# Turning f, q and k in separate parts, and one partial sum read by ScalarE: a change to a gated linear attention with an MLP on one core

## The chip, the cores and the metric

The kernel runs as one program on one core of a Trainium2 chip. The metric is the device time of one execution in microseconds; shorter is better. The core has five engines that run beside each other and wait for each other by semaphores: TensorE (PE in the profile, with PEld for its weight loads), VectorE (DVE), ScalarE (ACT), GpSimd (POOL) and SyncE (SP), which issues the transfers. Each engine works through its own list of instructions in order.

## The reference

```python
# q, k, v, f_logit: 4 batches x 8 heads x 768 tokens x 48
f = 1.0 / (1.0 + np.exp(-f_logit))
for t in range(S):
    state = f[:, :, t, :, None] * state + np.einsum('bhd,bhe->bhde', k[:, :, t], v[:, :, t])
    y[:, :, t] = np.einsum('bhd,bhde->bhe', q[:, :, t], state)
x = y.transpose(0, 2, 1, 3).reshape(B * S, H * D)     # 3072 tokens x 384
h = x @ w_in                                          # 384 x 2048
g = h * (1.0 / (1.0 + np.exp(-1.702 * h)))
out = g @ w_out                                       # 2048 x 384
```

Everything is float32.

## The kernel before

**Units.** The 3072 tokens are cut into 12 units of 256 tokens, three to a batch; the state is carried along within a batch. The attention of unit n+1 is computed while the MLP of earlier units runs. The MLP work lies in a list, `fill`, and `merge(n, fill, ...)` emits the parts of unit n's attention one after the other and, behind each part, as much of `fill` as the part's `share` says. A part kind with a share of 3 out of 19 is followed by 3/19 of that merge's MLP columns. In the merges 2 and 3 the same is done with the rest of the weights, which arrive as raw bits and are rebuilt by VectorE and ScalarE (`convert`, lines 208 to 228); there `converting` says how many of these instructions follow a part.

**A unit's attention.** For unit n >= 3 the inputs f, q and k of a unit come into the tile `raw` as they lie in memory. VectorE turns each of them (`turn`, line 327): f into `F`, on which ScalarE then computes the sigmoid (line 332), q into one of two places in `X`, k into the third place of `X`. `begin_f`, `begin` and `begin_k` do this; each then lets SyncE fetch the next unit's input (line 258). `begin` also has two small GpSimd copies (lines 357 and 358). `begin_k` has four instructions more: ScalarE copies half of k and half of q aside (`set_aside`, line 423, tiles `Kc` and `Qc`), VectorE multiplies the other halves in place by the gates (`promote`, line 439), and ScalarE copies the next `Kc`. `begin_gates` multiplies gates into `tot` on GpSimd (line 376); it has to wait for the previous unit's states, because `tot` is one buffer.

The parts of a unit in their order are: three parts "V" (scores of two levels each on TensorE, line 384; `promote`, masks on VectorE, line 410; the sums over v into the tile `y`, line 448), two parts "T" (k is turned back on TensorE, line 505, and copied to `kn` by ScalarE, line 506), one part "S" (the last sums into `y`, the products for the states, line 523, and the states `st` on VectorE, lines 538 to 543). The product of q with the states, line 563, is emitted at the head of the next unit's first part; its result is copied (`yT`, line 571) and sent into the MLP's input `xT`. Units 0 to 2 have six single levels "W" instead of the three "V". `parts_of(n)` places the turnings of unit n+1 among the parts of unit n.

**Who orders.** TensorE's order is that of the emission throughout. Up to the end of merge 3 the other engines' order is that of the emission too, but for instructions of later units that the scheduler puts in among the last of them. From merge 4 on a scheduler orders VectorE, ScalarE, GpSimd and SyncE.

**The MLP.** From unit 3 on, `mlp_unit` computes `h` (line 727, 16 tiles of 128 columns), the sigmoid (line 732) and the product `g` (line 733), then `mlp_o7` computes the output from seven products of quarters instead of eight. The seven products use four sums in PSUM, X, W, Y and Z, 128 x 192 each. X, Y and Z go on after they have been read once: the order is X, W, X, Y, Z, Y, Z, and p1, p4, p2, p6, p5, p7, p3 are what is done when each product is complete:

```python
def p6():
    nc.vector.tensor_tensor(row("u2"), t["p1"], t["Y"], ALU.add)
def p3():
    nc.vector.tensor_tensor(out_(0)[:, HC:], t["u2"], t["Z"], ALU.add)
    store(n, 0, out_(0))
```

The products h, o, the tkn of the parts "T" and the four sums share four PSUM buffers of the tag "mm". In the units 0 to 2 the MLP runs in blocks of four tiles: `mlp_block`, with o in line 755, its first sum copied by ScalarE (line 791) and the others added by VectorE (line 793).

Of the kernel before, what the change touches and what calls it, by code (L numbers as in the profile page):

```python
# [13 lines left out]
ALU = mybir.AluOpType  # L14
# [9 lines left out]
def kernel(  # L24
# [33 lines left out]
    nc = tc.nc  # L58
    B, H, S, D = q.shape
# [17 lines left out]
    N_FILL = 3  # L77
# [153 lines left out]
    def convert():  # L231

        if state["begin"] < len(pairs) and len(todo) <= NOP:
            begin_pair(state["begin"])
            state["begin"] += 1
        if todo and todo[0]:
            todo.pop(0)()
        if todo and todo[0] is None:
            todo.pop(0)
            state["done"] += 2  # L240
            fetch_weights()
# [34 lines left out]
    def load_vl(n, l):  # L276

        if n >= NALL:
            return
        t = vls[n, l] = ld.tile([P, DM], F32, tag=f"vl{l}", name=f"vl_{n}_{l}")  # L280
        if n < N_TURN:
            pt = ps.tile([P, DM], F32, tag="mm", name=f"tv_{n}_{l}", bufs=4)
            for g in range(NG):
                nc.tensor.matmul(
                    pt[g * 64:(g + 1) * 64], lhsT=perm[:, l - 1, :] if l else ident[:, ::2], rhs=vns[n][:, g, :],
                    start=True, stop=True,
                )
            nc.scalar.copy(t, pt)
            return
        nc.sync.dma_start(out=t, in_=v_toks[n % 2].rearrange("(n two m) e -> two n m e", two=2, m=LEV[l])[0])  # L290
# [315 lines left out]
    HF, HC = NFF // 2, DM // 2  # L606
    T = {}

    def quarter(w, i, j, ffs=slice(0, HF)):
        return w[:, i * HF + ffs.start:i * HF + ffs.stop, j * HC:(j + 1) * HC]  # L610
# [35 lines left out]
    def last_sum(n, g):  # L646

        for j in range(2):
            by = slice(0, G)
            nc.vector.tensor_tensor(g[j + 2][:, :, by], g[j + 2][:, :, by], g["S", j][:, :, by], ALU.subtract)  # L650

    def mlp_o7(n, g):
        a = lambda i, j: lambda f: g[j * 2 + f // FG][:, f % FG, i * G:(i + 1) * G]
        s = lambda i: lambda f: g["S", f // FG][:, f % FG, i * G:(i + 1) * G]
        b = lambda i, j: lambda f: quarter(w_out, i, j)[:, f]
        T_ = lambda i: lambda f: T[i][:, f] if i < 4 else T[4](f)
        t = {}

        def out_(tt):
            if "o" not in g:  # L660
                g["o"] = mlp.tile([P, U // P, DM], F32, tag="osb", name=f"osb_{n}", bufs=1)
            return g["o"][:, tt]

        def row(name):
            t[name] = mlp.tile([P, HC], F32, tag=name, name=f"{name}_{n}", bufs=1)
            return t[name]

        def p1():
            nc.scalar.copy(row("p1"), t["X"])

        def p4():
            nc.scalar.copy(row("p4"), t["W"])

        def p2():
            nc.scalar.copy(out_(0)[:, :HC], t["X"])
            last_sum(n, g)

        def p6():
            nc.vector.tensor_tensor(row("u2"), t["p1"], t["Y"], ALU.add)  # L679

        def p5():
            nc.scalar.copy(row("p5"), t["Z"])

        def p7():
            nc.vector.tensor_tensor(row("u3"), t["p1"], t["Y"], ALU.add)
            nc.vector.tensor_tensor(out_(1)[:, :HC], t["u3"], t["p4"], ALU.subtract)
            nc.vector.tensor_tensor(out_(1)[:, HC:], t["u3"], t["p5"], ALU.add)
            store(n, 1, out_(1))

        def p3():  # L690
            nc.vector.tensor_tensor(out_(0)[:, HC:], t["u2"], t["Z"], ALU.add)
            store(n, 0, out_(0))


        products = (
            ("X", a(0, 0), b(0, 0), p1, True), ("W", a(1, 1), T_(4), p4, True), ("X", a(0, 1), b(1, 0), p2, False),
            ("Y", s(0), T_(2), p6, True), ("Z", a(1, 0), T_(1), p5, True), ("Y", s(1), T_(3), p7, False),
            ("Z", a(0, 1), b(1, 1), p3, False),
        )

        def one(bank, lhs, rhs, done, new, f):
            if new and f == 0:
                t[bank] = ps.tile([P, HC], F32, tag="mm", name=f"o_{n}_{bank}", bufs=4)
            nc.tensor.matmul(  # L704
                t[bank], lhsT=lhs(f), rhs=rhs(f), start=(new and f == 0), stop=(f == HF - 1), skip_group_check=True,
            )
            if f == HF - 1:
                done()
        return [(HC, lambda p=p, f=f: one(*p, f), 0) for p in products for f in range(HF)]
# [53 lines left out]
    def store(n, tt, o):  # L763
        r0 = n * U + tt * P - 1
        nc.sync.dma_start(out=out[max(r0, 0):r0 + P, :], in_=o[1:] if r0 < 0 else o)
# [38 lines left out]
    def keep_up(times):  # L804

        if times:
            pt = ps.tile([P, NL * 64], F32, tag="mm", name=f"idle_{next(serial)}", bufs=4)
        for _ in range(times):
            nc.tensor.matmul(pt, lhsT=ident, rhs=masks.rearrange("p l t -> p (l t)"), start=True, stop=True)
# [4 lines left out]
    def parts_of(n):  # L814

        parts = list(units[n][1])
        _, inter = parts.pop()
        if n:
            kind, scores = parts[0]
            _, ahead = units[n - 1][1][-1]  # L820
            parts[0] = kind, lambda: (ahead(), scores())
        if n < N_TURN:

            def with_v(l):
                kind, fn = parts[l]
                return kind, lambda: (fn(), load_vl(n, l) if n == 0 or l else None, keep_up(2 * (n == 0 and l < 3)))
            parts[:NL] = [with_v(l) for l in range(NL)]
        if n + 1 < NALL:
            begin_f, begin, begin_k, begin_gates = units[n + 1][0]
            i = len(parts)  # L830
            if n + 1 < N_FILL:

                parts.append(("K", lambda: (begin_k(), begin_gates(), load_vl(n + 1, 0) if n + 1 < N_TURN else None)))
                parts.insert(i - 4, ("B", begin if n == 0 else lambda: None))
                parts.insert(i - 5, ("B", begin_f))
                if n:

                    kind, head = parts[0]
                    parts[0] = kind, lambda: (head(), begin())
            else:  # L840
                kind, states = parts.pop()
                parts += [("B", begin_k), (kind, lambda: (states(), begin_gates()))]
                parts.insert(i - 3, ("B", lambda: (begin_f(), begin())))
        else:
            parts.append(("W", inter))
        return parts

    def merge(n, fill, columns, share, pieces=0, hold=0, by=1.0, chores=()):

        parts = parts_of(n)
        total = sum(share(kind) for kind, _ in parts)
        converting = {"W": 3, "T": 3, "B": 1} if n < N_FILL - 1 else {"W": 3, "V": 4, "S": 3, "T": 1, "B": 1}
        total_ops = sum(converting.get(kind, 0) for kind, _ in parts)
        held = sum(share(kind) for kind, _ in parts[:hold])
        at = at_ops = done = ops = 0
        for kind, fn in parts:
            ready = state["done"]
            fn()  # L860
            for chore in chores[:2]:
                chore()
            chores = chores[2:]
            at += share(kind)
            at_ops += converting.get(kind, 0)
            n_ops = min(int(pieces * NOP * at_ops / (by * total_ops)), pieces * NOP) - ops
            ops += n_ops
            first, n_columns = done, max(0, columns * (at - held) / (total - held) - done)

            def some(end):  # L870
                nonlocal done
                while fill and done < end and fill[0][2] <= ready:
                    w, emit, _ = fill.pop(0)
                    emit()
                    done += w
            for i in range(n_ops):
                some(first + n_columns * i / n_ops)
                convert()
            some(first + n_columns)

    def steady(kind):
        return {"W": 3, "V": 4, "S": 3, "T": 1, "B": 1, "K": 1}.get(kind, 0)

    UNIT = NFF * NK * U + U // P * NFF * DM

# [12 lines left out]
    load_vn(1)  # L898
    fill = []
    merge(0, fill, 0, steady, 8)  # L900
    fill += mlp_blocks((0, 0)) + mlp_blocks((0, 1))
    merge(1, fill, UNIT // 2 - LAG // 2, steady, 10, hold=1)
# [40 lines left out]
```

## Time and profile before

| What | Value |
|---|---|
| Median of 4 runs (lowest to highest) | 658.35 us (656.14 to 659.15) |
| The profiled execution's time; its span | 658.86 us; 657.0 us |
| TensorE busy (PE) | 634.2 us, 97% of the span |
| TensorE weight loads (PEld) | 543.4 us, 83% |
| VectorE busy | 444.9 us, 68% |
| ScalarE busy | 229.9 us, 35% |
| GpSimd busy | 54.5 us, 8% |
| Mean granted TensorE clock | 0.997 |
| DMA | 67.67 MB, mean 103 GB/s |

Times in the text are microseconds from the start of the span unless they are durations. In the timeline a row has its start, the time from its first to its last instruction, the engine, the line, the operation, output and inputs, and how many instructions were merged into it; in square brackets stand the idle time of the engine before it and what ended that. Where two instructions of one engine follow each other, the second can start a little before the first one's recorded end, so the distance of two starts can be shorter than the duration. A float32 product shows as two MATMUL records.

### The profile page before, as it was taken

How to read it: one execution, taken by the hardware profiler on the slowest of the kernel's cores; microseconds unless marked ns; L12 is line 12 of the kernel's file. 1: busy time of each engine (PE TensorE's matmuls, PEld its weight loads, DVE VectorE, ACT ScalarE, POOL GpSimd, SP SyncE). 2: the span in 40 equal slices, each digit the busy share in tenths (PEclk: the TensorE clock that was granted, in tenths of full speed). 3: DMA queues.
4: the chain of work that ended last, by engine and by line, in shares of the span. 5: the costliest groups of instructions: out<-in, count | busy, mean ns of one | idle time of the engine just before them, and what ended most of it. 6: DMA issues, size and time to landing. Idle time of an engine off the chain costs nothing.

```text
span 657.0 us, 20397 instructions
## 1 busy us (share of the span) xinstructions
PE 634.2 (97%) x8958; PEld 543.4 (83%) x8958; DVE 444.9 (68%) x802; ACT 229.9 (35%) x477; POOL 54.5 (8%) x116
## 2 busy tenths in 40 slices
PE   6978989989999999999999999999999999999997
PEld 5656757766678689989989989989989989989997
DVE  2998967788887757657657658558558557553571
ACT  3465433243223423423324324324324324222120
POOL 3020020020001002002002002002002002000000
PEclk9999989999999999999999999999999999999999
DMA  8888865294125444524524524615614202101000
GB/s 185 209 220 215 208 144 130 77 222 81 44 58 153 133 107 109 149 54 118 146 46 121 143 49 120 160 31 119 166 27 103 67 25 62 40 2 26 25 1 24
DMA packets 67554, 67.67 MB, mean 103 GB/s; under 512 B 30410, under 2 KB 61290, under 8 KB 67466
## 3 DMA queue, kind: packets, MB, share of 16 engines
q1 hardware_dynamic: 67466, 66.38, 40.5%
q8 instruction: 70, 1.15, 0.8%
q14 instruction: 18, 0.15, 0.1%
HBM read 56.92 MB, written 8.65 MB: 100 GB/s over the span
## 4 chain that ended last, share of the span: by engine, by line
PE 84%; DVE 7%; DMA 5%; ACT 1%; issue 1%; SPq 1%; DVEq 0%; ACTq 0%
PE h L727 36%; PE o_Y L704 8%; PE o_X L704 7%; PE o L755 7%; PE o_Z L704 7%; PE sc L384 5%; PE y L448 4%; PE o_W L704 4%; DMA vn<-v_tok 2%; PE t L339 2%; PE y L563 2%; PE sc L523 1%; DMA bits<-in_moe_w_in_dram 1%; PE tkn L505 1%; DMA xT<-yT 1%; DVE s L219 1%
## 5 line engine op out<-in xcount | busy, mean ns | idle before, releaser
L727 PE MATMUL h<-xT,w_in 128*128 128x256 f32 (+1 forms) x1152 | 261.5, 383 | 6.8 <-DMA xT<-yT 4.2
L727 PEld LDWEIGHTS h<-xT,w_in 128*128 128x128 f32 x1152 | 216.5, 191 | 40.8 <-issue 3.9
L733 DVE TENSOR_TENSOR g<-h,sg 128x256 f32<-128x256 f32 (+1 forms) x192 | 80.9, 423 | 101.0 <-ACT sg L732 98.6
L732 ACT ACTIVATE sg<-h 128x256 f32<-128x256 f32 (+1 forms) x192 | 73.4, 384 | 195.9 <-PE h L727 190.9
L423 ACT COPY Kc<-X 128x512 f32<-128x512 f32 x69 | 46.2, 669 | 119.7 <-DVE X L439 84.8
L755 PE MATMUL o<-w_out,g 128*128 128x384 f32 x192 | 66.1, 493 | 0.0
L439 DVE TENSOR_TENSOR X<-X,tot 128x1024 f32<-128x1024 f32 x45 | 55.2, 1226 | 15.3 <-PE sc L384 10.2
L755 PEld LDWEIGHTS o<-w_out,g 128*128 128x128 f32 x192 | 35.3, 190 | 22.9 <-issue 1.4
L704 PE MATMUL o_X<-w_out,g 128*128 128x192 f32 x288 | 51.9, 329 | 0.0
L704 PE MATMUL o_Y<-T,S 128*128 128x192 f32 x288 | 51.1, 331 | 0.1
L704 PEld LDWEIGHTS o_Y<-T,S 128*128 128x128 f32 x288 | 46.5, 190 | 2.5 <-DVE u L679 1.2
L704 PEld LDWEIGHTS o_X<-w_out,g 128*128 128x128 f32 x288 | 47.3, 190 | 0.9
L410 DVE TENSOR_TENSOR A<-sc,masks 128x512 f32<-128x512 f32 x72 | 46.9, 682 | 0.0
L448 PE MATMUL y<-A,vl 64*48 64x64 f32 x2304 | 41.2, 217 | 0.5 <-issue 0.4
L376 POOL TENSOR_TENSOR tot<-F 128x512 f32<-128x512 f32 x12 | 12.5, 1040 | 348.0 <-DVE st L540 348.0
L448 PEld LDWEIGHTS y<-A,vl 64*48 64x48 f32 x2304 | 36.2, 120 | 4.0 <-issue 4.0
L327 DVE STREAM_TRANSPOSE X<-raw 128x1024 f32<-128x1024 f32 x18 | 36.7, 2039 | 2.4 <-PE y L563 2.4
L571 ACT COPY yT<-y 48x512 f32<-48x512 f32 x48 | 27.9, 580 | 12.7 <-PE y L563 12.2
L384 PEld LDWEIGHTS sc<-X,Kc 48*64 48x64 f32 x1344 | 24.1, 134 | 8.2 <-issue 3.2
L384 PE MATMUL sc<-X,Kc 48*64 48x64 f32 x1344 | 28.3, 220 | 1.8 <-DVE A L410 1.7
L376 POOL TENSOR_TENSOR tot<-tot 128x256 f32<-128x256 f32 (+4 forms) x60 | 27.1, 452 | 4.7
L704 PE MATMUL o_Z<-w_out,g 128*128 128x192 f32 x144 | 26.6, 331 | 0.0
(93 smaller groups left out, 658.4 us busy)
## 6 DMA issues: line engine op xcount, KB each, us to landing
vl<-v_tok SPq DMA_DIRECT2D x60, 192.0 KB, 3.0
bits<-in_moe_w_out_dram SPq DMA_DIRECT2D x8, 768.0 KB, 9.4
bits<-in_moe_w_in_dram SPq DMA_DIRECT2D x8, 576.0 KB, 7.8
v_tok<-in_v_dram SPq DMA_DIRECT2D x10, 384.0 KB, 4.3
vn<-v_tok SPq DMA_DIRECT2D x10, 384.0 KB, 7.1
xT<-yT SPq DMA_DIRECT2D x24, 144.0 KB, 2.8
raw<-in_q_dram SPq DMA_DIRECT2D x18, 192.0 KB, 4.2
raw<-in_f_logit_dram SPq DMA_DIRECT2D x18, 192.0 KB, 4.3
```

Source lines behind the costliest of these rows:

```text
L327: nc.vector.transpose(out.rearrange("p (a i j) -> p a j i", a=NP, j=R), raw[:, j].rearrange("p a (j d) -> p (a j) d", j=R)[:, :, :32],)
L376: nc.gpsimd.tensor_tensor(tn, t2[:, :, 0], t2[:, :, 1], ALU.mult)
L384: nc.tensor.matmul(out[g * HS:(g + 1) * HS, h, a, :], lhsT=lhs(h, a * U + g * G), rhs=rhs(h, a * U + g * G), start=True, stop=True,)
L410: nc.vector.tensor_tensor(A[:, :, c:c + w].rearrange("p h (x t) -> p h x t", t=64), t["sc"][:, :, c:c + w].rearrange("p h (x t) -> p h x t ...
L423: nc.scalar.copy(c.rearrange("p (n m) -> p n m", m=m), X[:, j, :NA].rearrange("p (n two m) -> p n two m", two=2, m=m)[:, :, hf, :],)
L439: nc.vector.tensor_tensor(qk, qk, by, ALU.mult)
L448: nc.tensor.matmul(dst(h, g, a), lhsT=vls[n, u][g * 64:(g + 1) * 64, (2 * a + h) * D:(2 * a + h + 1) * D], rhs=A(h, g, a), start=(start an ...
L704: nc.tensor.matmul(t[bank], lhsT=lhs(f), rhs=rhs(f), start=(new and f == 0), stop=(f == HF - 1), skip_group_check=True,)
L727: nc.tensor.matmul(ph, lhsT=w_in[:, c, ff * P:(ff + 1) * P], rhs=xTs[n][:, c, :], start=(c == 0), stop=(c == NK - 1))
L732: nc.scalar.activation(sg, ph, AF.Sigmoid, scale=1.702)
L733: nc.vector.tensor_tensor(g[ff // FG][:, ff % FG, :], ph, sg, ALU.mult)
L755: nc.tensor.matmul(t["po"], lhsT=g[ff // FG][:, ff % FG, tt * P:(tt + 1) * P], rhs=w_out[:, ff, :], start=(ff == ffs[0]), stop=(ff == ffs[ ...
```

## The change

The change has three edits.

- In `parts_of`, for the units from 3 on: before, f and q of the next unit were turned together in one part ahead of the first "T", and k in a part of its own ahead of the states. Now f is turned ahead of the first "T", q between the two "T", and k behind the states, as the last part of the merge.
- The shares and the places of the conversions follow: the part with the states has the new kind "S1" with share 1 and no conversions, and the k part the kind "K3" with share 3 and three conversions.
- In `mlp_o7`, p6 is a copy of Y by ScalarE into a tile "p6" instead of an addition by VectorE, and p3 adds p1 and Z and then p6, so that it has two additions instead of one.

```diff
         def p6():
-            nc.vector.tensor_tensor(row("u2"), t["p1"], t["Y"], ALU.add)
+            nc.scalar.copy(row("p6"), t["Y"])
...
         def p3():
-            nc.vector.tensor_tensor(out_(0)[:, HC:], t["u2"], t["Z"], ALU.add)
+            nc.vector.tensor_tensor(out_(0)[:, HC:], t["p1"], t["Z"], ALU.add)
+            nc.vector.tensor_tensor(out_(0)[:, HC:], out_(0)[:, HC:], t["p6"], ALU.add)
             store(n, 0, out_(0))
...
                 kind, states = parts.pop()
-                parts += [("B", begin_k), (kind, lambda: (states(), begin_gates()))]
-                parts.insert(i - 3, ("B", lambda: (begin_f(), begin())))
+                parts += [("S1", lambda: (states(), begin_gates())), ("K3", begin_k)]
+                parts.insert(i - 3, ("B", begin_f))
+                parts.insert(i - 1, ("B", begin))
...
-        converting = {"W": 3, "T": 3, "B": 1} if n < N_FILL - 1 else {"W": 3, "V": 4, "S": 3, "T": 1, "B": 1}
+        converting = {"W": 3, "T": 3, "B": 1} if n < N_FILL - 1 else {"W": 3, "V": 4, "S": 3, "T": 1, "B": 1, "K3": 3}
...
-        return {"W": 3, "V": 4, "S": 3, "T": 1, "B": 1, "K": 1}.get(kind, 0)
+        return {"W": 3, "V": 4, "S": 3, "T": 1, "B": 1, "K": 1, "S1": 1, "K3": 3}.get(kind, 0)
```

## The prediction, made before the changed kernel was run

> **What bounds the kernel.** First the busy shares of the page, then the windows (stretch, length, busy time and instruction count of each engine, clock).
>
> ```profile
> PE 634.2 (97%) x8958; PEld 543.4 (83%) x8958; DVE 444.9 (68%) x802; ACT 229.9 (35%) x477; POOL 54.5 (8%) x116
> ```
>
> ```profile
> 128.00:160.00 32.00, 28.41 (x318) 20.08 (x318) 28.40 (x49) 12.58 (x26) 3.75 (x8) 1.00 0.70 152
> 160.00:212.00 52.00, 52.00 (x569) 39.50 (x568) 40.75 (x73) 15.41 (x33) 3.57 (x8) 1.00 0.31 82
> 311.00:360.00 49.00, 49.00 (x775) 45.12 (x768) 32.94 (x52) 17.74 (x37) 4.56 (x8) 1.00 0.42 108
> ```
>
> TensorE is the bound at an undiminished clock (1.00), and the change takes nothing from its work. So only TensorE's stalls count: those of 128 to 160 (32.00 - 28.41 = 3.6 us) can be won, and from 160 on nearly every new one comes on top. The waits view (us in total, times, longest) names what the change touches:
>
> ```profile
> PE h L727 <- ACT kn L506: 1.3, 1, 1.3
> ...
> PEld y L563 <- DVE st L543: 2.6, 5, 0.8
> ...
> PEld o_Y L704 <- DVE u L679: 1.2, 4, 0.3
> ```
>
> **Where the change acts.** The built program's lists of instructions say more than the diff. In units 5 to 11 VectorE's list keeps k ahead of the states, as before; of the turnings only emission moves there, and the scheduler undoes it. The new place of k holds in the two merges whose order is that of the emission: merge 2 (k of unit 3, 120 to 160) and merge 3 (k of unit 4, 188 to 216). The sum has three terms and a tail.
>
> **1. p6, the MLP units beside merges 4 to 10.** The second product into Y waits until VectorE has added p1 and Y (L679), which stands behind a promotion (412.90 to 414.1). In the timeline of unit 6's MLP:
>
> ```profile
> 412.25 0.62 ACT L423 COPY Qc<-X 128x512 f32<-128x512 f32 x1
> ...
> 414.05 0.35 DVE L679 TENSOR_TENSOR u<-p,o_Y 128x192 f32<-128x192 f32 x1
> ...
> 414.44 2.57 PEld L704 LDWEIGHTS o_Y<-T,S 128*128 128x128 f32 x16 [0.28 <-DVE u L679]
> ```
>
> In the chain that ended last, seven such groups of 16 records take 2.87, 2.64, 2.87, 2.85, 2.69, 2.86 and 2.60; over 2.60 that is 1.18 in all, and the wait's row has 1.2. ScalarE's copy of a 128x192 sum takes 0.31 (L682); behind Qc's end at 412.87 it is done at 413.2, a microsecond before the product wants Y. Gain 1.2; nothing if the copy is queued behind the next Kc (ends 414.90, a loss of up to 0.5 in each of seven units, +3.5). VectorE gets one addition of 0.36 more per unit net, hidden in its 16 us of free time in the third window; ScalarE has more.
>
> **2. Merge 2.** The timeline before:
>
> ```profile
> 128.34 2.04 DVE L327 STREAM_TRANSPOSE F<-raw 128x1024 f32<-128x1024 f32 x1
> ...
> 131.70 0.58 ACT L506 COPY kn<-tkn 128x512 f32<-128x512 f32 x1
> ...
> 132.33 2.86 PE L727 MATMUL h<-xT,w_in 128*128 128x256 f32 x12 [1.32 <-ACT kn L506]
> ...
> 134.99 2.04 DVE L327 STREAM_TRANSPOSE X<-raw 128x1024 f32<-128x1024 f32 x1
> ...
> 139.57 0.68 ACT L423 COPY Kc<-X 128x512 f32<-128x512 f32 x1 [1.29 <-DVE X L439]
> ...
> 141.37 0.35 DVE L540 TENSOR_TENSOR st<-st,tot 128x192 f32<-128x192 f32 x1
> ...
> 145.16 0.68 PE L384 MATMUL sc<-X,Kc 48*64 48x64 f32 x32
> ```
>
> From the start of k's turning to the end of the second Kc, which the scores of level two need, it is 140.25 - 134.99 = 5.26 us; call this the k chain. Before, it runs ahead of the states, so the states are late. After, it runs behind them and the scores are late. The shares move two o products (4 records, 1.34) behind the states, so the F turning starts at 127.05 and kn is there 3.94 later as before, at 130.99; TensorE arrives at 130.36 and waits 0.63 instead of 1.32. It is through the sums for the states at 135.63. VectorE, by distances of starts (conversions 0.26 to 0.46, q's turning 1.88, now with the kn stretch behind it), starts the states at 136.5; eight at 0.39 end at 139.6. There k's turning starts, and the chain ends at 144.85. TensorE does the o products until 141.1, q with the states until 142.2, the level-one scores at once, and level two at 144.9 instead of 145.16: -0.3. The earlier place of a weight operation (L228) costs VectorE's backlog 0.46 against 0.4 won, and that backlog already stops TensorE twice here (0.76 at 154.8, 0.51 at 158.3). I take +0.1 net. Ends: -2.4 (the 3.6 us of stalls but for the first score) and +1.5 (full durations instead of distances: states end at 140.9, and the lateness reaches 158).
>
> **3. Merge 3.** Here before has no stall:
>
> ```profile
> 201.22 1.23 DVE L439 TENSOR_TENSOR X<-X,F 128x1024 f32<-128x1024 f32 x1 [1.29 <-ACT Qc L423]
> ...
> 203.07 0.37 ACT L732 ACTIVATE sg<-h 128x256 f32<-128x256 f32 x1
> ...
> 203.17 9.33 PE L727 MATMUL h<-xT,w_in 128*128 128x256 f32 x42
> ...
> 207.33 2.06 DVE L327 STREAM_TRANSPOSE F<-raw 128x1024 f32<-128x1024 f32 x1 [0.17 <-POOL tot L376]
> ...
> 209.22 0.41 DVE L733 TENSOR_TENSOR g<-h,sg 128x256 f32<-128x256 f32 x1
> ```
>
> After, TensorE ends the sums for the states at 200.5 (188.62 plus its records in the new order), the states are done at 203.3, a sum and one g follow, and k's turning starts at 204.1. ScalarE has the two copies and Kc ahead of the next sigmoid, which is ready 5.16 later at 209.3. VectorE's list has the promotion (207.4 to 208.7), then the turning of unit 5's F (2.06, to 210.7), then the g that this sigmoid feeds, done at 210.9. TensorE meanwhile takes four o records and five h tiles of 1.32, reaching the sixth at 208.4; that tile's PSUM buffer, one of four, comes free only by this g. Stall 210.95 - 208.4 = 2.55. Before, k's chain began 6.2 us earlier, its sigmoid was done at 203.44, and F's turning met a VectorE without arrears. I take +2.5. Ends: +1.3 without the F turning in front (g at 209.7), +3.5 by full durations; 0, if VectorE reaches k one microsecond earlier and F comes behind g. From 212 to 603 TensorE has no idle time to give it back.
>
> **Moved past queues.** Four k loads now stand on SyncE behind the vl and vn loads of the same merges; they land tens of us before their use, cost 0. q's two GpSimd copies (0.37 and 0.19) are needed only by the scores of the next unit: 0.
>
> **4. Tail.** The last unit's last store waits for L691 (653.67), and now a second dependent addition follows it. The nearest pair in the timeline:
>
> ```profile
> 651.07 0.36 DVE L685 TENSOR_TENSOR u<-p,o_Y 128x192 f32<-128x192 f32 x1 [4.78 <-PE o_Y L704]
> 651.52 0.36 DVE L686 TENSOR_TENSOR osb<-u,p 128x192 f32<-128x192 f32 x1
> ```
>
> L685 to L686, also dependent, is 0.45 from start to start: +0.4.
>
> [...]
>
> **Sum.** -1.2 + 0.1 + 2.5 + 0.4 = +1.8. The profiled execution takes 658.86, so 660.7; the median of the runs, 658.35, is 0.5 lower, so **660.2**, +0.28%. About 0.3%, 2.0 us, is what a measurement of this kernel can tell from no change: the bounds are 656.4 and 660.3, and the forecast stands at the upper one.
>
> **Rivals.**
> - Forecast (0.46): own range 659.0 to 661.6, half of it on each side of 660.3.
> - A, faster (0.22): the k chain is hidden in both merges. Sum -1.2 - 2.4 + 0 + 0.4 = -3.2, 655.1. It decides if k's turning starts within about 1.3 us of TensorE's end of the state sums in merge 2, and if in merge 3 g is done by 208.4. For it: the two late spots of before (2.43 from q-with-states to scores, 1.32 for kn) both have k's or q's turning in front. Against it: eight states stand between, 3.1 us.
> - B, slower (0.24): VectorE's backlog takes full durations. Merge 2 +1.5, merge 3 +3.5, -1.2 + 0.4: +4.2, 662.5. It decides if the first state of merge 2 starts after about 137.5. For it: VectorE is busy 28.40 of 32.00 there, and each lost microsecond goes into the waits at 154 and 158. Against it: F starts 1.3 earlier.
> - C, slower (0.06): p6 is queued behind Kc on ScalarE, so the steady gain is gone: +0.0 + 0.1 + 2.5 + 0.4 = +3.0, 661.4, and up to 3.5 more with the full loss. Against it: the copy stands directly behind Qc in ScalarE's list.
> - The change does not do what it says: for seven of nine turnings that is so already, and it is in the sum. What is left is 0.02, without a direction.
>
> **Numbers.** Faster: A, 0.22. Same: half the forecast and 0.01, 0.24. Slower: half the forecast, B, C and 0.01, 0.54. The range reaches from A (655.1) to just beyond B and short of C's full loss, 663.5.
>
> **Right or wrong in the profile after.** p6: the wait of o_Y for u is gone and the groups of 16 records take 2.60. Merge 2: L563 no longer waits for L543; the level-two scores wait for Kc instead, near 144.9. Merge 3: one wait of about 2.5 us of h for g of L733 between 207 and 212, with an F turning ahead of that g. Tail: two additions 0.45 apart behind the last product. Wrong if merge 3 shows no stall (then 657 to 658), or if stalls of merge 2's backlog grow beyond 1.3 in all.

## The result, and the profile after

The changed kernel is slower: 660.35 us in the median of 39 runs (656.97 to 664.35), beside 657.33 for before (654.90 to 660.51, 58 runs); the ratio is 1.0047, interval 1.0036 to 1.0058, that is +3.1 us (2.4 to 3.8). Measured once more beside two of the experiments it was 1.0035 (1.0019 to 1.0052). The prediction had 660.2, or +1.8 us, on a median of before of 658.35: sign and range hold, the size is short by more than a microsecond. That 660.2 lies so near 660.35 is luck: before ran 1.0 us faster in these runs than in the four that the forecast started from. The profiled execution took 659.39, its span 657.3.

Busy shares of the page and the three windows, after:

```profile
PE 634.4 (97%) x8958; PEld 544.6 (83%) x8958; DVE 443.7 (68%) x802; ACT 231.9 (35%) x486; POOL 58.9 (9%) x116
```

```profile
128.00:160.00 32.00, 29.79 (x436) 21.76 (x435) 26.39 (x48) 11.16 (x22) 3.36 (x8) 0.95 0.62 146
160.00:212.00 52.00, 49.36 (x424) 36.61 (x423) 36.86 (x66) 13.39 (x30) 3.18 (x8) 0.94 0.28 75
311.00:360.00 49.00, 49.00 (x782) 45.18 (x772) 32.75 (x52) 17.86 (x39) 4.56 (x8) 1.00 0.43 108
```

Work and steady units are as they were. The second window has lost its full TensorE (52.00 to 49.36), and two windows have lost their full clock (1.00 to 0.95 and 0.94). The loss of clock was in none of the prediction's terms. The waits view names the stalls; the wait of o_Y for u is no longer in it, and that of L563 for the states (L543) is down from 2.6 to 0.3:

```profile
PE h L728 <- DVE g L734: 2.6, 1, 2.6
...
PE sc L384 <- ACT Kc L423: 2.1, 2, 1.3
```

The timeline of merge 3, after (lines behind 691 have moved by one):

```profile
199.41 2.03 DVE L327 STREAM_TRANSPOSE X<-raw 128x1024 f32<-128x1024 f32 x1
...
202.72 1.23 DVE L439 TENSOR_TENSOR X<-X,F 128x1024 f32<-128x1024 f32 x1 [1.29 <-ACT Qc L423]
...
204.04 2.02 DVE L327 STREAM_TRANSPOSE F<-raw 128x1024 f32<-128x1024 f32 x1
...
205.92 0.72 DVE L734 TENSOR_TENSOR g<-h,sg 128x256 f32<-128x256 f32 x2
...
206.37 7.21 PE L728 MATMUL h<-xT,w_in 128*128 128x256 f32 x18 [2.64 <-DVE g L734]
```

That is the forecast chain: k's turning, promotion, unit 5's F, g, and then TensorE, which had waited 2.64. But its 18 records then take 7.21; the 30 records ahead of the stall take 6.64, at which pace 18 would take about 4. Windows of the same stretch show why (the column behind POOL is the granted clock):

```profile
203.00:206.00 3.00, 0.73 (x4) 0.30 (x2) 2.91 (x3) 1.22 (x3) 0.00 (x0) 0.96 1.00 225
206.00:209.50 3.50, 3.13 (x7) 2.53 (x8) 1.40 (x5) 1.76 (x4) 0.00 (x0) 0.50 0.08 25
209.50:213.00 3.50, 3.50 (x11) 2.80 (x10) 0.85 (x2) 0.61 (x2) 0.00 (x0) 0.56 0.03 10
```

For some seven microseconds, from just before the end of the stall on, the clock is at half, and from 206.37 on TensorE works at it. Merge 2 has a small case of the same, in the timeline after:

```profile
138.27 0.70 PE L384 MATMUL sc<-Qc,Kc 48*64 48x64 f32 x32 [0.68 <-ACT Qc L423]
140.23 0.70 PE L384 MATMUL sc<-X,Kc 48*64 48x64 f32 x32 [1.26 <-ACT Kc L423]
140.85 7.12 PE L756 MATMUL o<-w_out,g 128*128 128x384 f32 x16
```

```profile
140.90:144.30 3.40, 3.40 (x10) 1.89 (x7) 2.58 (x5) 2.29 (x5) 0.00 (x0) 0.50 0.95 260
```

Before, the 16 records of o took 5.43 (at 145.77).

**Comparing by stretches.** Executions differ by chance ahead of the changed merges: in before's profiled one TensorE waited 2.97 for xT and then ran at half clock for a time (below, a row of its timeline and a window), in after's it waited 0.35, up to 91.75.

```profile
94.67 6.67 PE L727 MATMUL h<-xT,w_in 128*128 128x256 f32 x22 [2.97 <-DMA xT<-yT]
```

```profile
96.00:100.00 4.00, 4.00 (x14) 3.28 (x13) 1.19 (x3) 0.77 (x2) 0.00 (x0) 0.68 0.47 101
```

So the traces are compared from the last single-level scores of merge 2 on, in five stretches: (1) to the level-two scores behind merge 2's end, (2) to the first scores of the second "V" of merge 3, (3) to q-with-states at the head of merge 4, (4) to the last product into Z, (5) to the end, which is known to 0.1 us. Before they take 24.78, 15.91, 51.36, 438.44 and 6.13 us. By the built programs' lists, a changed merge 2 has two o products more in stretch 1 (1.34), a changed merge 3 has one h tile less in 2 and one more in 3 (1.33); this is taken out below. For after, stretch 3 is 58.62 - 1.33 - 51.36 = +5.93. All numbers are differences to before, in us:

| Kernel | 1 | 2 | 3 | 4 | 5 | sum | ratio of times (interval) |
|---|---|---|---|---|---|---|---|
| after | -0.37 | +0.08 | +5.93 | -1.27 | +0.49 | +4.9 | 1.0047 (1.0036 to 1.0058) |
| after_again | -0.40 | -0.99 | +2.87 | -1.27 | +0.47 | +0.7 | 1.0035 (1.0019 to 1.0052) |
| p6_alone | -0.01 | +0.01 | 0.00 | -1.25 | +0.43 | -0.8 | 0.9983 (0.9968 to 0.9998) |
| turnings_alone | -0.38 | -0.97 | +4.55 | -0.03 | +0.04 | +3.2 | 1.0041 (1.0019 to 1.0063) |
| merge3_as_before | -0.39 | -1.39 | 0.00 | -1.27 | +0.48 | -2.6 | 0.9979 (0.9965 to 0.9994) |
| the same again | -0.37 | -0.63 | 0.00 | -1.26 | +0.50 | -1.8 | 0.9983 (0.9961 to 1.0005) |
| merge2_as_before | 0.00 | +0.52 | +4.30 | -1.26 | +0.49 | +4.1 | 1.0062 (1.0039 to 1.0084) |
| stall_filled | -0.38 | -0.42 | +2.90 | -1.26 | +0.50 | +1.3 | 1.0041 (1.0023 to 1.0058) |
| the same again | -0.39 | -0.89 | +2.90 | -1.26 | +0.45 | +0.8 | 1.0013 (0.9997 to 1.0028) |
| F_behind_g | -0.41 | -0.49 | +1.91 | -1.10 | +0.48 | +0.4 | 1.0011 (0.9988 to 1.0034) |
| apart_k_ahead | -0.02 | -0.01 | -0.03 | -1.09 | +0.43 | -0.7 | 0.9997 (0.9976 to 1.0019) |

The sum is one execution, the ratio the median of several; 0.1% is 0.66 us. How far one execution's stretch 2 can be off by chance is shown by merge2_as_before: +0.52 with merge 2 as before. The 2.90 of stall_filled in stretch 3 holds 2.66 of repeated work.

### The profile page after: what moved, and what is told of

Same layout as the page of the kernel before. It is cut to its first block, busy times and chain, and to the rows that moved or that the text cites. A ratio compares the mean times of both kernels' runs of the same rounds, so it can differ in the third digit from the quotient of the medians.

```text
span 657.3 us, 20407 instructions
## 1 busy us (share of the span) xinstructions
PE 634.4 (97%) x8958; PEld 544.6 (83%) x8958; DVE 443.7 (68%) x802; ACT 231.9 (35%) x486; POOL 58.9 (9%) x116
## 4 chain that ended last, share of the span: by engine, by line
PE 83%; DMA 6%; DVE 4%; ACT 2%; SPq 2%; issue 1%; DVEq 0%; ACTq 0%
PE h L728 36%; PE o_X L705 7%; PE o_Y L705 7%; PE o_Z L705 7%; PE o L756 6%; PE sc L384 5%; PE y L448 4%; DMA bits<-in_moe_w_in_dram 4%; PE o_W L705 4%; PE y L563 2%; DMA xT<-yT 2%; PE sc L523 1%; PE tkn L505 1%; ACT yT L571 1%; DVE X L327 1%
## 5 line engine op out<-in xcount | busy, mean ns | idle before, releaser
L756 PE MATMUL o<-w_out,g 128*128 128x384 f32 x192 | 67.9, 503 | 0.0
L685 DVE TENSOR_TENSOR u<-p,o_Y 128x192 f32<-128x192 f32 x9 | 3.2, 354 | 37.2 <-PE o_Y L705 37.2
```

Of the source, the lines that this page charges most:

```text
L756: nc.tensor.matmul(t["po"], lhsT=g[ff // FG][:, ff % FG, tt * P:(tt + 1) * P], rhs=w_out[:, ff, :], start=(ff == ffs[0]), stop=(ff == ffs[ ...
```

## The experiments

**The parts one by one.** p6_alone is before with the third edit only; turnings_alone is the changed kernel without it; the other two put one merge back:

```diff
+                if n == 3:        # merge3_as_before; n == 2 in merge2_as_before
+                    parts += [("B", begin_k), (kind, lambda: (states(), begin_gates()))]
+                    parts.insert(i - 3, ("B", lambda: (begin_f(), begin())))
+                else:
                     parts += [("S1", lambda: (states(), begin_gates())), ("K3", begin_k)]
...
```

p6_alone:

> The kernel before with only the third edit (p6 a copy by ScalarE, p3 with two additions). The theory (the parts add up: steady units -1.2, tail +0.4 to +0.5, the rest of the change in merges 2 and 3): 0.7 to 0.8 us faster than before, -0.1%; from the first product q with the states of merge 4 to the last product into Z about 437.2 us instead of 438.4, and no wait of o_Y for VectorE. Rival (the copy is late on ScalarE, or the extra VectorE addition delays g): equal or up to 2 us slower, with that stretch unchanged or longer. Second rival (the whole loss of 3 us sits in the tail and the units): 3 us slower.

Measured: 655.07 against 656.15, 0.9983 (0.9968 to 0.9998). Stretch 4 takes 437.19, the tail 6.56 instead of 6.13; both terms of the theory hold. VectorE has 802 instructions in all before and after, ScalarE 477 and 486: each of nine units moves one operation, and p3's added addition takes the place of p6's. In the timeline of the changed kernel, unit 6's MLP:

```profile
412.69 0.61 ACT L423 COPY Qc<-X 128x512 f32<-128x512 f32 x1
...
413.21 0.30 ACT L679 COPY p<-o_Y 128x192 f32<-128x192 f32 x1
...
414.72 2.76 PE L705 MATMUL o_Y<-T,S 128*128 128x192 f32 x16
```

The copy is done 1.2 us ahead of the product. At the end, also after:

```profile
653.48 0.35 DVE L691 TENSOR_TENSOR osb<-p,o_Z 128x192 f32<-128x192 f32 x1 [1.46 <-PE o_Z L705]
653.87 0.36 DVE L692 TENSOR_TENSOR osb<-osb,p 128x192 f32<-128x192 f32 x1
```

The second addition follows 0.39 behind the first.

turnings_alone:

> The changed kernel with p6 and p3 as before, so only the turnings, shares and conversions are changed. The theory (the loss is the stall of merge 3 and the half clock behind it, paid back in part by p6): slower than before by 3 + 0.8 = 3.8 us, +0.6%; stall of h for g near 2.6 in merge 3, then some microseconds at a granted clock of 0.5; q with the states of merge 4 to the last product into Z 438.4 again. Rival (the parts do not add, p6 causes part of the loss by moving ScalarE's queue in merge 3): 2 us slower or less.

Measured: 658.75, +0.41% (+1.2 to +4.1 us). The stall is 2.64 again, stretch 4 is 438.41 again. By the stretches the parts add up. The times neither confirm nor refute it: -0.17% and +0.41% make +0.24%, for +0.47% and +0.35%, and the interval holds both the theory's 3.8 us and the rival's 2.

merge3_as_before, run twice:

> The changed kernel, but the parts of merge 3 are in the order of before (unit 4's f and q turned together, k ahead of the states); merge 2 and the later merges and p6 are as changed. The theory (stall and half clock are merge 3's and cost 2.6 + up to 3.4): the stall is gone, 0.5 to 1.5 us faster than before. Rival (most of the loss comes from merge 2, where the two waits of the scores also bring the clock down for 3.5 us): still 2 us or more slower than before.

> merge3_as_before once more, for the direct comparison with yT_first and to see whether it is faster than before a second time. Theory (merge 2's new order and p6 gain about 1.2 us each by the stretches, the loss was merge 3's): 1 to 2.5 us faster than before again, no stall in merge 3. Rival (its first result was the lucky end of its interval): within 0.7 us of before.

Measured: 654.55 and 654.97, 0.9979 and 0.9983 (the second interval reaches 1.0005). The stall is gone and stretch 3 is 51.36 to the hundredth: the whole loss, and more, is merge 3's. Against the changed kernel this is 4.5 us by the two first ratios and 3.4 us by the two later ones, above the 2.64 of the stall. Against p6_alone (0.9983) the times show no gain: what merge 2 adds is seen in the stretches alone.

merge2_as_before:

> The changed kernel, but the parts of merge 2 are in the order of before (unit 3's f and q together, k ahead of the states). The theory (merge 2 is worth about nothing, -0.3 to 0 us): 3 us slower than before, as the changed kernel, with merge 3's stall of 2.6 and the half clock behind it. Rival (merge 2 carries half of the loss): 1 to 1.5 us slower than before. Rival two (merge 2's new order gains what was forecast at most, 2.4 us): 5 us slower.

Measured: 659.91, +0.62% (+2.6 to +5.5 us). This lies above the changed kernel's +0.47%, though the intervals overlap; in the stretches merge 2's new order is worth -0.4 in 1 and between +0.1 and -1.4 in 2. That it is worth about nothing, as the theory has it, is not borne out by the stretches.

**Is it the stall or the clock behind it?** The stall was 2.64 in all four profiled executions that keep it as it is. These are the 18 records behind it in turnings_alone, merge2_as_before and after_again:

```profile
205.56 5.84 PE L727 MATMUL h<-xT,w_in 128*128 128x256 f32 x18 [2.64 <-DVE g L733]
```

```profile
209.39 5.59 PE L728 MATMUL h<-xT,w_in 128*128 128x256 f32 x18 [2.64 <-DVE g L734]
```

```profile
207.14 4.15 PE L728 MATMUL h<-xT,w_in 128*128 128x256 f32 x18 [2.64 <-DVE g L734]
```

With after's 7.21: one stall, and 0 to 3.06 us on top of it. The 4.15 ran at a clock of 1.00, the others had it at 0.50 for about 3.4 us, or 6.8 in after. stall_filled lets TensorE compute the tile ahead of the stall three times into the same PSUM buffer, 2.66 us of repeated work, and changes nothing else:

```diff
+        times = lambda ff: 2 if (n, ff) == (2, 12) else 0
...
+            (NK * U, lambda ff=ff: [one(ff, c, i, times(ff)) for i in range(times(ff) + 1) for c in range(NK)],
```

> The changed kernel, but in merge 3 TensorE computes the h tile ahead of the stall (unit 2, columns 12) three times instead of once into the same PSUM buffer, so that the 2.6 us in which it waited for g are filled with 2.66 us of its own work at the same place; VectorE, ScalarE and their order are untouched. Theory (a stall of 2.6 us costs more than its length, since the granted clock falls to 0.5 for 3.5 to 7 us behind it): no row under 1.00 behind 204, and 1.7 to 3.4 us faster than the changed kernel, 0 to 1.3 us slower than before. Rival (the clock does not follow from the stall, or the loss is only the wait): no faster than the changed kernel, 3 us slower than before.

> The changed kernel once more, for the direct comparison with the two beside it and a second look at its clock. Theory (merge 3's stall of 2.6 us drags the clock to 0.5 for one or two stretches of 3.5 us): again 3 us slower than before, stall 2.6 and a half clock behind it for 3.5 or 7 us. Rival (the half clock was one execution's accident): the stall with a clock of 1.00 behind it.

> The kernel stall_filled once more, now beside the changed kernel itself, since the profiles put it 1.4 to 3.0 us below the kernels with the stall between merge 3's first scores and merge 4, and the medians of the two did not show that. Theory (the half clock is paid in every execution with the stall): 1.5 us or more faster than the changed kernel beside it. Rival (in the timed executions the clock does not matter): the same time as the changed kernel within 0.7 us.

In both profiled executions of stall_filled the clock is 1.00 behind 204; the windows, first and second time:

```profile
204.00:212.00 8.00, 7.92 (x37) 6.55 (x35) 5.46 (x8) 3.99 (x9) 0.00 (x0) 1.00 0.47 113
```

```profile
204.00:212.00 8.00, 7.92 (x36) 6.40 (x35) 5.46 (x8) 3.84 (x9) 0.00 (x0) 1.00 0.44 109
```

Stretch 3 is 55.59 in both; with the stall it is 58.62, 57.24, 56.99 and 55.56. The medians are less clear. The first time stall_filled's ratio to the before beside it (1.0041) was no better than the changed kernel's to another before (1.0047), which speaks for the rival; the second time, side by side, it was 656.87 against 658.52, 1.65 us faster, with intervals that just overlap. The trace of after_again came out as its rival said, with the stall and a clock of 1.00, but over the four traces the half clock is no accident of one execution: it stands in three.

How much of it the timed runs pay stays open. Their mean granted clock was lower with the stall where kernels with and without it were measured side by side, but by little: 0.9954 in after_again and 0.9968 in stall_filled_again, 0.9944 in turnings_alone and 0.9954 in merge3_as_before. That is 0.9 and 0.7 us of full clock per run (difference times 655). Before has 0.9972 over 106 runs beside the experiments, the 39 first runs of the changed kernel 0.9931. A run's mean does not tell merge 3's half clock from merge 2's, or from one ahead of both: merge3_as_before, without the stall, has the same 0.9954 as after_again.

**What sets the stall's length.** F_behind_g emits unit 5's F turning at the end of merge 3:

```diff
+                parts.insert(i - 3, ("B", (lambda: None) if n == 4 else begin_f))
...
+                if n == 3:
+                    parts.append(("F", units[5][0][0]))
```

> The changed kernel, but unit 5's F is turned at the end of merge 3, behind the g products there, instead of ahead of the g that TensorE waits for. Theory (the F turning in front is 0.9 to 1.3 us of the stall, the k chain the rest): the stall shrinks from 2.64 to 1.4 to 1.7, and the drop of the clock becomes rarer or shorter: 1 to 3 us faster than the changed kernel. Rival (the k chain alone sets it): the stall stays 2.6 and the time stays 3 us above before. Rival two (the F turning is then late for the units behind): a new wait behind 215 that gives back the gain.

Its timeline:

```profile
203.17 1.23 DVE L439 TENSOR_TENSOR X<-X,F 128x1024 f32<-128x1024 f32 x1 [1.27 <-ACT Qc L423]
...
205.39 0.76 DVE L734 TENSOR_TENSOR g<-h,sg 128x256 f32<-128x256 f32 x2 [0.99 <-ACT sg L733]
205.87 4.15 PE L728 MATMUL h<-xT,w_in 128*128 128x256 f32 x18 [1.67 <-DVE g L734]
```

The stall is 1.67, so the F turning was 0.97 of it and the k chain the rest; no half clock followed here (the clock is 1.00 up to 220), and TensorE's rows from 215 to 220 show no new wait. 656.49, +0.11% (-0.8 to +2.2 us): below the changed kernel by 2.4 us by its first ratio and 1.6 by its second, more than the 0.97, as the theory says, but with intervals that overlap.

**Parting f and q, or k behind the states?** apart_k_ahead has f and q apart in merges 2 and 3, but k ahead of the states:

```diff
+                if n in (2, 3):
+                    parts += [("B", begin_k), (kind, lambda: (states(), begin_gates()))]
...
```

> The changed kernel, but in the merges 2 and 3 k stays ahead of the states (with the shares of before for these two parts) while f and q are turned apart as changed. Theory (the place of k behind the states makes merge 3's stall, the parting of f and q does not): no stall in merge 3; in merge 2 the wait for kn is halved as in the changed kernel, the states are late again as before; about as merge3_as_before, 0.5 to 2 us faster than before. Rival (parting f and q costs too, q's turning being now directly in front of k's): 1 us or more slower than merge3_as_before.

Measured: 654.65, 0.9997 (0.9976 to 1.0019); stretches 1 to 3 are as before within 0.03. So with k ahead of the states, parting f and q does nothing, for or against: in merge 2 the wait for kn falls from 1.32 to 0.46, and 1.11 of waiting for the states comes before L563 instead of 0.18. Both what merge 2 gains and what merge 3 loses come from the place of k, with the shares and conversions that move with it; these were not tested by themselves. The expectation that merge 2 keeps a gain was wrong in that.

**Two versions that were to beat merge3_as_before.** Both put o products between q-with-states and the scores at the head of merge 3, under which the k chain can end; yT_first also emits the copies of yT ahead of those of the k chain, which `late_k` holds back:

```diff
             if n == 3:
-                parts[0] = kind, lambda: (ahead(), scores())
+                parts.insert(0, ("B", ahead))                            # o_before_scores
+                parts.insert(0, ("A", lambda: (ahead(), late_k[n]())))   # yT_first, share 1.8
```

> A version drawn from the runs: merge3_as_before, and at the head of merge 3 the products of q with unit 2's states stand as a part of their own with a share of 1, so that some o products (3.4 us) lie between them and unit 3's first scores, under which the k chain of unit 3 can end. Theory (in merge 2 of the changed kernel the scores wait 0.6 for Qc and 1.3 for the second Kc and this can halve the clock behind them): both waits gone, no half clock behind 140, 2 to 3 us faster than merge3_as_before, 3 to 4.5 us faster than before. Rival (VectorE's backlog in that stretch takes the place of the waits, since its conversions and g products are late anyway): the waits come back as waits of h for sums or g between 145 and 160, no faster than merge3_as_before.

> A second version drawn from the runs: merge3_as_before with the o products between q-with-states and the scores as in o_before_scores (here all eight, 5.4 us), and unit 3's k chain cut in two: its turning stays behind the states, its ScalarE copies and its promotion are emitted behind the copies of yT of unit 2. Theory (in o_before_scores the 2.5 us wait of h for xT came from the three copies of the k chain ahead of the yT copies on ScalarE): yT is done at about 143.6 instead of 146.4, so xT lands near 148, just behind the scores; waits between 136 and 152 under 1 us in all and no half clock there; the stretch from the last single level of merge 2 to the first scores behind merge 3's head part 2 to 2.5 us shorter than in o_before_scores, 2 to 4 us faster than before, 1 to 2.5 us faster than merge3_as_before beside it. Rival (a third wait takes the place: VectorE's conversions stand ahead of the promotion, so the second Kc is late): scores wait 1 us or more for Kc and the time is that of merge3_as_before.

Measured: 656.20, 0.9996 (0.9977 to 1.0015), and 656.11, 0.9998 (0.9979 to 1.0018). By the ratios both are slower than merge3_as_before, by 1.1 us (first ratio of it) and 1.0 us (second), where they were to be faster. The scores wait no more in either, but the h tiles behind them do. One row of o_before_scores, then one of yT_first:

```profile
150.69 9.33 PE L728 MATMUL h<-xT,w_in 128*128 128x256 f32 x42 [2.53 <-DMA xT<-yT]
```

```profile
149.50 12.22 PE L731 MATMUL h<-xT,w_in 128*128 128x256 f32 x48 [4.08 <-DMA xT<-yT]
```

In yT_first y ends at 138.96 and its h starts at 149.50: 10.5 us for copies, issues and landing, with 6.5 us of o and scores to do meanwhile. In merge3_as_before the same way takes 9.2 us (140.01 to 149.22) and holds the two waits of the scores, 0.68 and 1.25. Those waits lay under the way of xT; taken away, they come back as a wait for it. The texts of o_before_scores did not name this wait; yT_first was to remove it and made it longer. Its copies do end earlier, at 141.47, ahead of the 143.6 hoped for. What takes longer is the transfer: the h tile whose wait ends with xT starts 8.1 us behind the first issue of xT at 141.40, against 4.9 in merge3_as_before (issue at 144.28) and in o_before_scores (145.80). That issue stands 1.2 us behind that of a load of weights (L180), against 3.0 in merge3_as_before, and the DMA engines are busy for 96% and more of every 2 us from 140 to 148. That the transfer queues behind these weights fits, but was not tested.

## Why the prediction was right in sign and short in size

- **p6: right.** -1.25 to -1.27 in stretch 4 for -1.2 in eight of the ten executions of the table with the new p6 (-1.10 and -1.09 in F_behind_g and apart_k_ahead). The copy stands directly behind Qc and is done at 413.51, for 413.2; the groups of the second product into Y take 2.60. One statement was wrong, at no cost: "VectorE gets one addition of 0.36 more per unit net". p6 gives one up where p3 takes one on, and VectorE's 802 instructions stay.
- **Tail: right.** +0.43 to +0.50 for +0.4. The second addition takes 0.36, as the row of L686 did before, and starts 0.39 behind the first, for the 0.45 from L685 to L686.
- **Merge 2: the waits right, the gain too small.** Set on one zero (after is 4.56 us ahead by chance), the level-two scores start at 140.23 + 4.56 = 144.79 for 144.9, and stretch 1 gained 0.4 for 0.3. The level-one scores were to start "at once"; they waited 0.68 for Qc, and the level-two scores started when forecast all the same. Stretch 2 was to lose it again. It gained about 1 where the clock behind the scores stayed at 1.00 (-0.97, -0.99, -0.89, and -1.39 and -0.63 in merge3_as_before), and +0.1 to -0.5 where it fell. The failed step is "The earlier place of a weight operation (L228) costs VectorE's backlog 0.46 against 0.4 won, and that backlog already stops TensorE twice here": both stops of before (0.76 and 0.51) are gone after, and a wait of h for xT has come instead, of 0.3 to 1.3 in six of the eight executions with the new merge 2; in the other two, stall_filled and F_behind_g, the o products ahead of it ran at half clock and no wait is left. The mean over the eight is -1.1 for both stretches, for a term of +0.1.
- **Merge 3: the stall right, its price not.** 2.64 for 2.55, one wait, with the F turning ahead of the g, and 0.97 of F in it for the 1.25 between the two ends. The failed step is "I take +2.5", behind "Stall 210.95 - 208.4 = 2.55": it prices a stall at its length. Stretch 3 lost 2.87, 4.30, 4.55 and 5.93, in the mean 4.4: the 2.87 is the stall and 0.23 more at a full clock, what goes beyond it is time at half clock. The trace of before showed such a case: its wait of 2.97, which ends at 94.67, is followed by a window at a clock of 0.68 (96 to 100). It lay outside the changed merges and was not read.
- **Sum.** With the means of the traces: -1.25 + 0.47 - 1.1 + 4.4 = +2.5, for the measured +3.1 and +2.3. The misses of merge 2 (1.2 too high) and merge 3 (1.9 too low) partly cancel in the forecast's +1.8.
- **Rivals.** A (hidden in both merges) failed in merge 3, and in merge 2 k's turning started 3.7 us behind the end of the state sums (131.19 and 134.93), not within 1.3. B (full durations, +4.2) is about as near the measured +3.1 as the forecast, but not for its reason: the first state of merge 2 starts at 131.88 + 4.56 = 136.4, ahead of its 137.5. VectorE kept the distances, and the clock paid the difference. That seven of nine turnings stay in place on VectorE's list fits stretch 4 of turnings_alone (-0.03).

The half clock followed the stall of 2.64 three times in four, and in merge2_as_before it also followed a wait of 1.71 that ended at 92.33. In after the clock is 0.50 from 140.9 to 144.3 and from 205.8 to 212.6, that is for 3.4 and 6.8 us.

## What to carry to other kernels

A stall of the bound engine can have a second price, here 0 to 3.06 us on top of 2.64: look in the trace of before for a wait of the same length and read the clock of the windows behind it. One trace gives no certain price: of waits alike in length some were followed by the half clock (1.71 in merge2_as_before) and others not (1.73 in p6_alone). One move (k behind the states) can win in one stretch and lose in the next; put in only where it won, with p6, it made a version 0.2% below before (the second interval just reaches no change) and 0.5 to 0.7% below the changed kernel. By time p6 alone is as fast (0.9983); that merge 2 adds to it is seen in the stretches only. A wait that is removed should be checked for a second one beneath it, such as the wait for xT here, of 2.53 and 4.08 us where those of the scores were gone.

## What was not expected of the hardware

The same stall of 2.64 us was followed by no, one or two stretches of about 3.4 us at a granted clock of 0.50, so that two executions of one program, after and after_again, differ by 3.06 us in stretch 3 (+5.93 and +2.87). Two waits of 0.68 and 1.26 us, 0.7 us apart, were enough for one such stretch in three of the eight profiled executions that have them in merge 2. Of the waits of h for xT, one of 4.08 (yT_first), one of 2.97 (before) and one of 1.71 (merge2_as_before) were followed by the half clock; one of 2.53 (o_before_scores), one of 2.44 (merge3_as_before) and one of 1.73 (p6_alone) were not: here the length of a wait below 3 us did not tell what followed. Behind 2.66 us of repeated products in the gap the clock stayed at 1.00 both times; the gap itself left it at 1.00 once in four, so two executions are few.
